# A planned one-core attention and mixer kernel: four small edits to its start, one wait, its normalisation and its last tile

## The chip, the cores and the metric

The kernel runs on one core of one Trainium2 chip. The metric is the device time of one execution in microseconds (us). A profile of an execution has a *span*, from the first to the last recorded instruction; the device time is longer than the span by 1.7 to 2 us in most runs. The engines are called PE (TensorE matrix products), PEld (its weight loads), DVE (VectorE), ACT (ScalarE), POOL (GpSimd) and SP (the queue that issues most transfers).

## The reference, cut to what matters

```python
# x: 2048 x 448, H = 16 heads of 28, N = 4 segments of L = 512 tokens, F = 1792
phi = lambda t: where(t > 0, t + 1, exp(t))
for s in range(4):
    qs, ks, vs = q[:, :, s], k[:, :, s], v[:, :, s]
    a_dot = softmax(qs @ ks.T * scale + causal_mask) @ vs
    a_mem = (phi(qs) @ M) / (phi(qs) @ z + 1e-6)      # memory of the earlier segments
    outs.append(g * a_mem + (1 - g) * a_dot)
    M, z = M + phi(ks).T @ vs, z + phi(ks).sum(...)
a = concat(outs) @ wo
u = gelu(layernorm(x).T @ w1 + b1)                    # mixes tokens: (448 x 2048) @ (2048 x 1792)
b = (u @ w2 + b2).T
out = gate * a + (1 - gate) * b                       # gate = sigmoid((x * gate_w).sum(-1))
```

## The kernel before

The kernel carries a small planner. Every instruction is registered with the engine that it may run on, a told cost in nanoseconds, a priority, and the buffers that it reads and writes. `plan()` simulates this list with the told costs and fixes, before anything runs, the order of instructions on every engine, which of two engines takes an instruction that has an `alt`, and which PSUM bank a result goes to. On the chip every engine then issues strictly in that order and waits on semaphores. So any edit to a cost, a dependency or the list of instructions can change the order of the whole program. PSUM banks 0 to 3 belong to the attention scores (after the start), banks 4 to 7 are a pool that all other products share.

```python
# start: x in tiles of 128 tokens; the first four make segment 0
load_x("SP", 0, 2)
load_x("ACT", 2, 2)
op("ACT", ... dma_start(wvx[.., D:D+1], gate_w ..), name="ldgw", ...)      # 448 elements of 2 bytes
op("SP",  ... dma_start(wk_nat, WK ..), name="ldwk", ...)
# ... cut: wq, wv, the other x tiles
warm_up(10, "warm", -1, 4300)                    # 128x512 products of zeros
warm_up(4, "warm2", P_PROJ + 0.01, 900, 5000.0)
# ... cut

def transposes(tc):                              # x^T of 512 tokens
    for half in range(2):                        # two of the four column blocks each
        # 8 PE transposes into one bank, then one copy of 1024 columns:
        # on DVE for half 0, on ACT for half 1 where tc == 0

def do_k(tc, hg):                                # k of 4 heads, 512 tokens, 4 matmuls of 512
    proj_d(wk_pad, R_wkp, hg, tc, b)
    op("ACT", ... copy of 512 columns ..., alt=("DVE", ...))
```

An attention unit is one segment and one group of four heads, each padded from 28 to 32 columns. Its scores come in three parts, f = 0, 1, 2, each followed by an exponential on ACT and a mask on POOL.

```python
def pv_unit(u):
    mb, cb = Bank("pool"), Bank("pool")
    if s > 0:                                    # phi(q) @ memory, into a pool bank
        op("PE", ... matmul(bank(mb)[:, 0:512], mst_sb[:, s-1, hg, :], phq[...]) ...,
           reads=[R_mst[s - 1], R_phq[hg][s]], writes=[bres(mb)], take=mb, name=f"mem{u}", ...)
    op("PE", fn, reads=R_P[tb] + R_v[...], take=cb, name=f"pv{u}", ...)      # exp(scores) @ v
    # DVE transposes mb and cb out of PSUM into t2; then, on all 32 columns of each head:
    dv(... t3[0] = t3[0] * oc * rb[0] ..., "oa", 668)          # 512 elements
    dv(... t3[1] = t3[1] * rb[1] ..., "om", 601)
    op("POOL", ... o = t2[:,0] + t2[:,1] ..., cost=1450)

def mm2(T):                                      # one output tile of 128 tokens
    for ft in range(NFT):                        # 14 matmuls of 448 columns
        op("PE", ... matmul(bank(b)[:, 0:D], w2c[...], uT[:, ft, :]) ...)
    op("DVE", ... outst = bank * omg + ag(T) ..., name=f"fin{T}", cost=600)  # the eviction
    op("SP", ... dma_start(out2[T*128 : T*128+128, :], outst[:, p, :]) ...)
```

The softmax here doesn't subtract the row's maximum and nothing guards it: scores larger than these inputs give would overflow.

## Time and profile before

| what | value |
|---|---|
| time | 190.52 us, median of 3 (190.13 to 190.76) |
| span of the profile | 189.0 us |
| first k projection starts | 8.28 us |
| last eviction starts | 186.15 us |
| between these two ("the middle") | 177.87 us |
| from the last eviction's start to the end of the span ("the tail") | 2.85 us |

Part 1 of the page gives each engine's busy time, its share of the span and its count of instructions:

```profile
PE 181.4 (96%) x1349; PEld 84.7 (45%) x1355; DVE 155.7 (82%) x311; ACT 136.2 (72%) x171; POOL 74.3 (39%) x93
```

PE is the limit. The timeline shows the start (columns: start, duration, engine, line, operation, shapes, count, and in brackets the idle time before it and what ended that):

```profile
start us, us, engine line op out<-in xcount [idle before <-releaser]
...
1.25 4.45 PE L524 MATMUL t<-t 128*128 128x512 bf16 x10 [1.25 <-DVE t L478]
...
5.49 1.59 PE L551 MATMUL t<-t 128*112 128x128 bf16 x16
...
6.91 1.03 PE L524 MATMUL t<-t 128*128 128x512 bf16 x4
7.11 1.02 ACT L563 ACTIVATE t<-t 112x1024 bf16<-112x1024 bf16 x1 [3.98 <-PE t L551]
...
8.28 1.02 PE L572 MATMUL t<-t 112*128 112x512 bf16 x4 [0.34 <-ACT t L563]
```

Ten warm-up matmuls, 16 transposes and four more warm-up matmuls run one after the other, then PE waits 0.34 us for ACT's long copy. The timeline of PE alone, after the first projection, is nearly gapless. These are all its lines with a wait, except two (60.66 and 128.73 us) that show 0.16 us of "issue" and no releaser:

```profile
30.75 0.39 PE L765 MATMUL t<-t 28*128 28x512 bf16 x4 [0.52 <-ACT t L774]
...
34.03 0.40 PE L765 MATMUL t<-t 28*128 28x384 bf16 x8 [0.48 <-ACT t L642]
...
38.00 0.36 PE L870 MATMUL t<-t 128*128 128x448 bf16 x1 [0.18 <-ACT t L584]
38.91 0.39 PE L765 MATMUL t<-t 28*128 28x512 bf16 x4 [0.55 <-ACT t L774]
...
105.77 0.73 PE L870 MATMUL t<-t 128*128 128x448 bf16 x3 [0.57 <-DVE t L670]
```

Four waits between 30 and 39 us are for ScalarE: 0.52 + 0.48 + 0.18 + 0.55 = 1.73 us. Scores (L765) can't be computed until the exponential (L774) has emptied the four score banks. One wait, at 105.8 us, is for VectorE's L670, which prepares the memory that a memory matmul (L788) multiplies with. The records of 6 of the 12 memory matmuls are missing in this trace, though their weight loads are there, and a missing record looks like idle time. One is missing just before 105.77 us, and one before each of the two "issue" lines, which are therefore not waits. A later run with the same order of PE, only_last_tile, has all records and shows the wait as it is:

```profile
105.34 0.39 PE L788 MATMUL t<-t 128*128 128x512 bf16 x1 [0.34 <-DVE t L670]
```

So PE waits 1.73 + 0.34 = 2.07 us in all. The table of stretches, for 24 to 40 us:

```profile
core 0: us, PE busy (x) PEld busy (x) DVE busy (x) ACT busy (x) POOL busy (x), PEclk, DMA share, GB/s
24.00:40.00 16.00, 14.27 (x102) 5.66 (x101) 15.03 (x40) 14.33 (x22) 9.44 (x12) 1.00 0.39 62
```

The PE timeline from 146 us also has this line; it shows three memory matmuls in a row, which take three of the four pool banks at once:

```profile
149.45 0.82 PE L788 MATMUL t<-t 128*128 128x512 bf16 x3
```

And the end, in the timeline:

```profile
174.79 11.32 PE L898 MATMUL t<-t 128*128 128x448 bf16 x59
...
186.15 0.68 DVE L904 SCALAR_TENSOR_TENSOR t<-t 128x448 bf16<-128x448 f32 x1 [1.96 <-PE t L898]
```

After the last matmul an eviction of 0.68 us and one transfer remain.

### The profile page before, as it was taken

Reading aid. Unit: us, or ns where it says so; the run is one execution under the profiler, and the core shown is the slowest. Engines: PE = TensorE matmul, PEld = TensorE weight load, DVE = VectorE, ACT = ScalarE, POOL = GpSimd, SP = SyncE. Lnnn points to the kernel's source line nnn. Section 1 sums busy time; section 2 is a strip of 40 time slices with the busy share of each in tenths; the row PEclk is TensorE's granted clock in tenths of the full one; section 3 lists DMA queues with packets and bytes.
Section 4 is the critical chain, followed back from the end, with each engine's and each line's share of the span. In section 5 each row is a group of like instructions: output and inputs, shape, how many; then the busy total and the mean of one; then the engine's idle time right before and its main releaser. Section 6 shows DMA issues by size and latency. Waiting matters only on the chain.

```text
span 189.0 us, 3425 instructions
## 1 busy us (share of the span) xinstructions
PE 181.4 (96%) x1349; PEld 84.7 (45%) x1355; DVE 155.7 (82%) x311; ACT 136.2 (72%) x171; POOL 74.3 (39%) x93
## 2 busy tenths in 40 slices
PE   7999998889999999999999899999999999999993
PEld 2545633334445444434445344444446444455551
DVE  1788899895999999899989998997998997872221
ACT  2276988986899989999998899986757867204100
POOL 8200027645242528364447454274570075510000
PEclk9999999999999999999999999999999999999999
DMA  5899991000955271801081514405590016655011
GB/s 163 208 318 243 294 204 28 0 3 0 245 120 140 70 183 28 222 7 28 0 225 43 152 28 121 105 24 127 147 270 1 3 51 192 176 150 164 26 49 49
DMA packets 42451, 21.75 MB, mean 115 GB/s; under 512 B 7876, under 2 KB 42436, under 8 KB 42436
## 3 DMA queue, kind: packets, MB, share of 16 engines
q1 hardware_dynamic: 41700, 21.32, 43.9%
q10 hardware_dynamic: 736, 0.23, 0.5%
q8 instruction: 10, 0.16, 0.4%
q14 instruction: 5, 0.04, 0.1%
HBM read 18.13 MB, written 1.84 MB: 106 GB/s over the span
## 4 chain that ended last, share of the span: by engine, by line
PE 80%; DVE 12%; ACT 6%; issue 1%
PE t L898 23%; PE t L870 20%; PE t L572 10%; PE t L850 7%; PE t L765 6%; PE t L628 5%; PE t L802 4%; ACT t L774 3%; PE t L524 2%; DVE t L714 2%; PE t L551 1%; ACT t L613 1%; DVE t L817 1%; DVE t L562 1%; PE t L652 1%
## 5 line engine op out<-in xcount | busy, mean ns | idle before, releaser
L774 ACT ACTIVATE t<-t 128x2048 bf16<-128x2048 f32 (+1 forms) x48 | 76.7, 1597 | 10.8 <-PE t L765 9.7
L778 POOL TENSOR_SCALAR_AFFINE_SELECT t<-t 128x512 bf16<-128x512 bf16 x64 | 49.1, 772 | 83.0 <-ACT t L774 79.9
L870 PE MATMUL t<-t 128*128 128x448 bf16 x224 | 48.0, 354 | 0.8 <-DVE t L670 0.6
L898 PE MATMUL t<-t 128*128 128x448 bf16 x224 | 45.3, 353 | 0.3 <-issue 0.2
L898 PEld LDWEIGHTS t<-t 128*128 128x128 bf16 x224 | 20.9, 98 | 20.8 <-issue 1.5
L572 PE MATMUL t<-t 112*128 112x512 bf16 x128 | 29.8, 380 | 0.3 <-ACT t L563 0.3
L870 PEld LDWEIGHTS t<-t 128*128 128x128 bf16 x224 | 20.1, 98 | 20.6 <-issue 2.5
L904 DVE SCALAR_TENSOR_TENSOR t<-t 128x448 bf16<-128x448 f32 x16 | 10.9, 679 | 14.4 <-PE t L898 14.3
L830 POOL TENSOR_TENSOR t<-t 128x512 bf16<-128x512 f32 x12 | 16.5, 1372 | 11.5 <-DVE t L828 11.5
L765 PE MATMUL t<-t 28*128 28x512 bf16 (+3 forms) x256 | 17.3, 302 | 1.7 <-ACT t L774 1.1
L572 PEld LDWEIGHTS t<-t 112*128 112x128 bf16 x128 | 11.7, 97 | 14.9 <-issue 1.0
L856 ACT ACTIVATE t<-t 128x448 bf16<-128x448 f32 x12 | 8.7, 723 | 12.3 <-PE t L850 11.9
L628 PE MATMUL t<-t 112*128 112x449 bf16 x64 | 13.5, 355 | 0.0
L765 PEld LDWEIGHTS t<-t 28*128 28x128 bf16 x256 | 5.1, 92 | 18.3 <-ACT t L774 12.3
L850 PE MATMUL t<-t 128*128 128x448 bf16 x64 | 13.3, 353 | 0.0
L836 DVE STREAM_TRANSPOSE t<-t 128x512 bf16<-128x512 bf16 x16 | 11.2, 701 | 1.7 <-POOL t L830 1.7
L817 DVE STREAM_TRANSPOSE t<-t 128x512 f32<-128x512 f32 x16 | 11.0, 698 | 1.5 <-PE t L802 1.5
L714 DVE BATCH_NORM_STATS2 t<-t 128x6 f32<-128x448 bf16 x16 | 9.4, 607 | 3.0 <-DMA t<-in_A_x_dram 2.9
L802 PE MATMUL t<-t 128*32 128x512 bf16 (+3 forms) x256 | 11.3, 302 | 0.1
L826 DVE SCALAR_TENSOR_TENSOR t<-t 128x512 f32<-128x512 f32 x12 | 11.1, 921 | 0.1
L595 DVE SCALAR_TENSOR_TENSOR t<-t 128x512 bf16<-128x512 bf16 x12 | 10.1, 845 | 0.0
L882 DVE SCALAR_TENSOR_TENSOR t<-t 128x448 f32<-128x448 f32 x14 | 8.8, 641 | 1.1 <-ACT t L877 1.1
(80 smaller groups left out, 215.6 us busy)
## 6 DMA issues: line engine op xcount, KB each, us to landing
t<-in_B_w_dram SPq DMA_DIRECT2D x7, 1024.0 KB, 6.2
t<-in_B_w_dram SPq DMA_DIRECT2D x8, 896.0 KB, 5.2
out_dram<-t SPq DMA_DIRECT2D x16, 112.0 KB, 2.3
t<-in_A_x_dram SPq DMA_DIRECT2D x3, 448.0 KB, 9.3
t<-in_A_wk_dram SPq DMA_DIRECT2D x1, 392.0 KB, 5.1
t<-in_A_wq_dram SPq DMA_DIRECT2D x1, 392.0 KB, 7.1
t<-in_A_wv_dram SPq DMA_DIRECT2D x1, 392.0 KB, 8.4
t<-in_A_wo_dram SPq DMA_DIRECT2D x4, 98.0 KB
```

The source lines that it names most:

```text
L572: last = e.matmul(bank(b)[:, 0:512], w_pad[0:CK, c, hg * 128 : hg * 128 + 128], xT[0:CK, c, tc * 512 : tc * 512 + 512], start=(c == 0), st ...
L628: last = e.matmul(bank(b)[:, 0 : D + 1], xT[0:CK, c, t * 128 : t * 128 + 128], wvx[0:CK, c, :], start=(c == 0), stop=(c == NCT - 1), skip_ ...
L714: op("DVE", lambda e: e.bn_stats(st6[:, t, :], xh[:, t, :]), reads=[R_x[t]], writes=[R_st6[t]], name=f"bns{t}", cost=512, prio=P_PROJ - 10)
L765: last = e.matmul(bank(hl)[:, c0 : c0 + w_], kT[r, hg, s * 512 + j * 128 : s * 512 + j * 128 + 128], qT[r, hg, s * 512 + 128 * j : s * 512 ...
L774: op("ACT", lambda e: e.activation(pv, ps[:, 0:4, 0:w], ACT.Exp, scale=SCALE), reads=R_bank[0:4], writes=[R_P[u % 2][f]], name=f"exp{n}", ...
L778: op("POOL", lambda e, d=d: e.affine_select(d, d, pattern=[[0, 4], [1, 128]], compare_op=ALU.is_ge, fill=0.0, base=0, channel_multiplier=- ...
L802: last = e.matmul(bank(cb)[32 * hl : 32 * hl + 32, 128 * j : 512], vaug[:, 4 * s + j, 32 * h : 32 * h + 32], pv[:, hl, c0 : c0 + w_], star ...
L817: dv(lambda e: e.transpose(t2[:, 0, :], bank(cb)[:, 0:512]), [bres(cb)], [R_tt[tb][0]], "ta", 630, use=(cb,))
L830: op("POOL", lambda e: e.tensor_tensor(o, t2[:, 0, :], t2[:, 1, :], op=ALU.add), reads=R_tt[tb], writes=[R_ob[tb]], name=f"o{u}", cost=145 ...
L850: last = e.matmul(bank(b)[:, 0:D], oT[:, hg, T * 128 : T * 128 + 128], wo_sb[:, hg, :], start=(hg == 0), stop=(hg == NHG - 1), skip_group_ ...
L870: op("PE", lambda e, st=st: e.matmul(bank(b)[:, 0:D], w1c[:, st, f2 * 128 : f2 * 128 + 128], xh[:, st, :], start=(st == 0), stop=(st == NT ...
L898: op("PE", lambda e, ft=ft: e.matmul(bank(b)[:, 0:D], w2c[:, ft, t2_ * 128 : t2_ * 128 + 128], uT[:, ft, :], start=(ft == 0), stop=(ft == ...
```

## The change

It has four parts.

- **A, the start.** wk is loaded ahead of x tiles 2 and 3, which move from ACT's queue to SP's. The transposes of segment 0 go by token half, and so do the copies and the k projections (two of 256 tokens, for each head group). One warm-up matmul fewer. The intent is that the first projections need only half of x.
- **B, one line.** The memory matmul also "reads" the second exponential of its unit, so that it isn't planned long before its bank will be emptied.
- **C, head pads.** Normalisation works on 28 of each 32 columns, 448 of 512 elements; the pads of `ob` are cleared once. The told costs fall with it.
- **D, last tile.** The last output tile is computed, evicted and stored in two halves of 224 columns, so that the final eviction and transfer are smaller.

```diff
 A    load_x("SP", 0, 2)
-     load_x("ACT", 2, 2)
+     op("SP", ... dma_start(wk_nat ..), name="ldwk", ...)
+     load_x("SP", 2, 2)
      ...
-     warm_up(4, "warm2", P_PROJ + 0.01, 900, 5000.0)
+     warm_up(3, "warm2", P_PROJ + 0.01, 680, 4000.0)
      ...   # transposes(0): parts ordered by token half; 512-column copies, three on DVE, one on ACT
-     for hg in range(NHG):
-         do_k(0, hg)
+     for t0 in (0, 256):
+         for hg in range(NHG):
+             do_k(0, hg, t0, 256)

 B    # memory matmul
-        reads=[R_mst[s - 1], R_phq[hg][s]], ...
+        reads=[R_mst[s - 1], R_phq[hg][s], R_P[tb][1]], ...

 C    # normalisation
+     op("DVE", ... memset(warm[:, 512:1024], 0.0), writes=[R_ob[1]], name="ob0", ...)
-     o3 = o.rearrange("p (b c) -> p b c", c=32)
+     o3 = o.rearrange("p (b c) -> p b c", c=32)[:, :, 0:DH]
+     n3 = [t[:, :, 0:DH] for t in t3]
-     ... "oa", 668 ...  "om", 601 ...  cost=1450
+     ... "oa", 602 ...  "om", 535 ...  cost=1280

 D    def mm2(T, c0=0, c1=D): ...       # columns c0:c1, own resource for the second half
+     def mm2_last(T):
+         mm2(T, 0, D // 2)
+         mm2(T, D // 2, D)
```

More of the change, by code (lines that the diff above doesn't have):

```diff
@@ L404, in build_kernel @@
     R_xT = [R(f"xT{t}_", 2) for t in range(4)]
+    R_xT0 = [R(f"xT0h{h}_", 2) for h in range(2)]
+    R_xT[0] = R_xT0[0] + R_xT0[1]
     R_phk = [R(f"phk{s}_", NHG) for s in range(3)]
@@ L410, in build_kernel @@
     R_kT = [R(f"kT{g}_", 4) for g in range(NHG)]
+    R_kTh = R("kTh", NHG)
     R_phq = [R(f"phq{g}_", 4) for g in range(NHG)]
@@ L418, in build_kernel @@
     R_rec = R("rec", 2)
-    R_ob, R_outst = R("ob", 2), R("outst", 4)
+    R_ob, R_outst = R("ob", 2), R("outst", 5)
     R_P = [R(f"P{u}_", 3) for u in range(2)]
@@ L435, in build_kernel @@
     load_x("SP", 0, 2)
-    load_x("ACT", 2, 2)
+    op("SP", lambda e: e.dma_start(wk_nat[0:CK], WK.rearrange("(c p) d -> p c d", p=CK)), writes=R_P[0],
+       name="ldwk", dma=True, cost=500, nbytes=401408)
+    load_x("SP", 2, 2)
     op("ACT", lambda e: e.dma_start(wvx[0:CK, :, D : D + 1], GW.rearrange("(c p o) -> p c o", p=CK, o=1),
@@ L439, in build_kernel @@
        writes=[R_gw], name="ldgw", dma=True, cost=500, nbytes=8000)
-    op("SP", lambda e: e.dma_start(wk_nat[0:CK], WK.rearrange("(c p) d -> p c d", p=CK)), writes=R_P[0],
-       name="ldwk", dma=True, cost=500, nbytes=401408)
     op("SP", lambda e: e.dma_start(wq_nat[0:CK], WQ.rearrange("(c p) d -> p c d", p=CK)), writes=R_P[1],
@@ L474, in ring_load @@
                writes=[R_slot[r]], name=f"ldw2_{j}", dma=True, cost=500, nbytes=917504)
+    P_BASE, P_ATT, P_PROJ, P_WO, P_M1, P_M2 = 0.0, 100.0, 200.0, 300.0, 400.0, 500.0
+    PRJ = (P_PROJ, P_PROJ + 1, P_M1 + 8.5, P_M2 + 4.5)
+    REL0, REL = 0.0, 0.0
     warm = ob.rearrange("p a q -> p (a q)")
     op("DVE", lambda e: e.memset(warm[:, 0:512], 0.0), writes=[R_ob[0]], name="warm0", cost=250)
+    op("DVE", lambda e: e.memset(warm[:, 512:1024], 0.0), writes=[R_ob[1]], name="ob0", cost=250, prio=P_PROJ)
     op("POOL", lambda e: e.memset(ident[:], 1.0), writes=[R_ident], name="id0", cost=200)
@@ L503, in load_wo @@
                reads=[R_wv], writes=[R_wo[hl]], name=f"ldwo{hl}", dma=True, cost=500, nbytes=100352)
-    P_BASE, P_ATT, P_PROJ, P_WO, P_M1, P_M2 = 0.0, 100.0, 200.0, 300.0, 400.0, 500.0
-    PRJ = (P_PROJ, P_PROJ + 1, P_M1 + 8.5, P_M2 + 4.5)
-    REL0, REL = 0.0, 0.0
     rr = [0]
@@ L543, in transposes, with fn @@
             b = next_bank()
-            def fn(e, half=half, b=b):
+            parts = [(ti, c) for ti in range(4) for c in (2 * half, 2 * half + 1)]
+            if tc == 0:
+                parts = [(ti, c) for c in range(4) for ti in (2 * half, 2 * half + 1)]
+            def fn(e, b=b, parts=parts):
                 tb = bank(b).bitcast(BF16)
                 last = None
-                for ti in range(4):
-                    for c2 in range(2):
-                        c = half * 2 + c2
-                        last = e.matmul(tb[0:CK, c2 * 512 + ti * 128 : c2 * 512 + ti * 128 + 128],
-                                        xh[:, 4 * tc + ti, c * CK : c * CK + CK], ident[:, :], is_transpose=True,
-                                        start=True, stop=True, skip_group_check=True)
-                return last
@@ L556, in io @@
-            def io(half=half, b=b):
-                return (xT[0:CK, 2 * half : 2 * half + 2, tc * 512 : tc * 512 + 512],
-                        bank(b).bitcast(BF16)[0:CK, :].rearrange("p (c t) -> p c t", c=2))
-            op("PE", fn, reads=R_x[4 * tc : 4 * tc + 4] + [R_ident], writes=[bres(b)], **btake(b),
-               name=f"trx{tc}_{half}", mode="f", cost=8 * 56, prio=P_PROJ)
-            on_dve = ("DVE", lambda e, io=io: e.tensor_copy(*io()), dve_cost(1024, 2))
-            on_act = ("ACT", lambda e, io=io: e.activation(*io(), ACT.Copy), act_cost(1024))
@@ L564, in transposes @@
-            first, other = (on_act, on_dve) if tc == 0 and half == 1 else (on_dve, on_act)
-            op(first[0], first[1], **buse(b), reads=[bres(b)], writes=[R_xT[tc][half]], name=f"xTcp{tc}_{half}",
-               cost=first[2], prio=P_PROJ + tc - 150, alt=other if tc else None)
-    def proj_d(w_pad, R_w, hg, tc, b):
+                for ti, c in parts:
+                    at = (c * 256 + ti % 2 * 128) if tc == 0 else (c % 2 * 512 + ti * 128)
+                    last = e.matmul(tb[0:CK, at : at + 128], xh[:, 4 * tc + ti, c * CK : c * CK + CK], ident[:, :],
+                                    is_transpose=True, start=True, stop=True, skip_group_check=True)
@@ new lines, in fn, with io @@
+                return last
+            op("PE", fn, reads=[R_x[4 * tc + ti] for ti, c in parts] + [R_ident], writes=[bres(b)], **btake(b),
+               name=f"trx{tc}_{half}", mode="f", cost=8 * 56, prio=P_PROJ + (0.02 if tc == 0 and half else 0))
+            if tc == 0:
+                for k, on_dve in ((0, True), (1, half == 1)):
+                    def io(b=b, half=half, k=k):
+                        return (xT[0:CK, 2 * k : 2 * k + 2, half * 256 : half * 256 + 256],
+                                bank(b).bitcast(BF16)[0:CK, k * 512 : k * 512 + 512].rearrange("p (c t) -> p c t", c=2))
+                    if on_dve:
+                        op("DVE", lambda e, io=io: e.tensor_copy(*io()), reads=[bres(b)], writes=[R_xT0[half][k]],
+                           name=f"xTcp0_{half}{k}", cost=dve_cost(512, 2), prio=P_PROJ - 150)
+                    else:
+                        op("ACT", lambda e, io=io: e.activation(*io(), ACT.Copy), reads=[bres(b)],
+                           writes=[R_xT0[half][k]], name=f"xTcp0_{half}{k}", cost=act_cost(512), prio=P_PROJ - 150)
+            else:
+                def io(half=half, b=b):
+                    return (xT[0:CK, 2 * half : 2 * half + 2, tc * 512 : tc * 512 + 512],
+                            bank(b).bitcast(BF16)[0:CK, :].rearrange("p (c t) -> p c t", c=2))
+                op("DVE", lambda e, io=io: e.tensor_copy(*io()), **buse(b), reads=[bres(b)], writes=[R_xT[tc][half]],
+                   name=f"xTcp{tc}_{half}", cost=dve_cost(1024, 2), prio=P_PROJ + tc - 150,
+                   alt=("ACT", lambda e, io=io: e.activation(*io(), ACT.Copy), act_cost(1024)))
@@ L569, in fn, with proj_d @@
+    def proj_d(w_pad, R_w, hg, tc, b, t0=0, n=512):
         def fn(e):
@@ L571, in fn, with do_k @@
             for c in range(NCT):
-                last = e.matmul(bank(b)[:, 0:512], w_pad[0:CK, c, hg * 128 : hg * 128 + 128],
-                                xT[0:CK, c, tc * 512 : tc * 512 + 512], start=(c == 0), stop=(c == NCT - 1),
+                last = e.matmul(bank(b)[:, 0:n], w_pad[0:CK, c, hg * 128 : hg * 128 + 128],
+                                xT[0:CK, c, tc * 512 + t0 : tc * 512 + t0 + n], start=(c == 0), stop=(c == NCT - 1),
                                 skip_group_check=True)
             return last
-        op("PE", fn, reads=R_xT[tc] + [R_w], writes=[bres(b)], **btake(b), name=f"prd{tc}_{hg}", mode="f",
-           cost=pe_cost(512, 512, 512, 512), prio=PRJ[tc])
-    def do_k(tc, hg):
+        need = R_xT[tc] if tc else [r for h in range(2) if t0 < 256 * h + 256 and t0 + n > 256 * h for r in R_xT0[h]]
+        op("PE", fn, reads=need + [R_w], writes=[bres(b)], **btake(b), name=f"prd{tc}_{hg}", mode="f",
+           cost=pe_cost(n, n, n, n), prio=PRJ[tc] + (0.01 if t0 else 0))
+    def do_k(tc, hg, t0=0, n=512):
         b = next_bank()
-        ks = kT[:, hg, tc * 512 : tc * 512 + 512]
-        proj_d(wk_pad, R_wkp, hg, tc, b)
-        op("ACT", lambda e: e.activation(ks, bank(b)[:, 0:512], ACT.Copy),
-           **buse(b), reads=[bres(b)], writes=[R_kT[hg][tc]], name=f"cpk{tc}_{hg}", cost=act_cost(512), prio=P_BASE,
-           alt=("DVE", lambda e: e.tensor_copy(ks, bank(b)[:, 0:512]), dve_cost(512)))
+        ks = kT[:, hg, tc * 512 + t0 : tc * 512 + t0 + n]
+        proj_d(wk_pad, R_wkp, hg, tc, b, t0, n)
+        op("ACT", lambda e: e.activation(ks, bank(b)[:, 0:n], ACT.Copy),
+           **buse(b), reads=[bres(b)], writes=[R_kTh[hg] if t0 else R_kT[hg][tc]], name=f"cpk{tc}_{hg}",
+           cost=act_cost(n), prio=P_BASE, alt=("DVE", lambda e: e.tensor_copy(ks, bank(b)[:, 0:n]), dve_cost(n)))
     def do_kphi(tc, hg):
@@ L590, in do_kphi @@
         ks = kT[:, hg, tc * 512 : tc * 512 + 512]
-        op("ACT", lambda e: e.activation(kphi[:, p, :], ks, ACT.Exp), reads=[R_kT[hg][tc]],
+        op("ACT", lambda e: e.activation(kphi[:, p, :], ks, ACT.Exp), reads=[R_kT[hg][tc]] + ([] if tc else [R_kTh[hg]]),
            writes=[R_kphi[p]], name=f"ek{tc}_{hg}", cost=act_cost(512, True), prio=P_PROJ + tc)
@@ L769, in fn @@
             return last
-        op("PE", fn, reads=[R_kT[hg][s], R_qT[hg][s]], writes=R_bank[0:4], name=f"sc{n}", mode="r",
+        op("PE", fn, reads=[R_kT[hg][s], R_qT[hg][s]] + ([] if s else [R_kTh[hg]]), writes=R_bank[0:4], name=f"sc{n}", mode="r",
            cost=w / 2.4 + 17, prio=pr, rel=REL0 + REL * u)
@@ L790, in pv_unit @@
                                         skip_group_check=True),
-               reads=[R_mst[s - 1], R_phq[hg][s]], writes=[bres(mb)], take=mb, name=f"mem{u}", mode="f",
+               reads=[R_mst[s - 1], R_phq[hg][s], R_P[tb][1]], writes=[bres(mb)], take=mb, name=f"mem{u}", mode="f",
                cost=pe_cost(512), prio=pr)
@@ L820, in pv_unit @@
         o = ob[:, tb, :]
-        o3 = o.rearrange("p (b c) -> p b c", c=32)
-        rb = [rec[:, tb, k, :, None].to_broadcast([128, 16, 32]) for k in range(2)]
+        o3 = o.rearrange("p (b c) -> p b c", c=32)[:, :, 0:DH]
+        n3 = [t[:, :, 0:DH] for t in t3]
+        rb = [rec[:, tb, k, :, None].to_broadcast([128, 16, DH]) for k in range(2)]
         oc = omcol[:, hg : hg + 1]
@@ L825, in pv_unit @@
             dv(lambda e: e.reciprocal(rec[:, tb, :, :], dens), R_tt[tb], [R_rec[tb]], "rec", 280)
-            dv(lambda e: e.scalar_tensor_tensor(t3[0], t3[0], oc, rb[0], op0=ALU.mult, op1=ALU.mult),
-               [R_tt[tb][0], R_rec[tb], R_omcol], [R_tt[tb][0]], "oa", 668, port=True)
-            dv(lambda e: e.tensor_tensor(t3[1], t3[1], rb[1], op=ALU.mult), [R_tt[tb][1], R_rec[tb]], [R_tt[tb][1]],
-               "om", 601, port=True)
-            op("POOL", lambda e: e.tensor_tensor(o, t2[:, 0, :], t2[:, 1, :], op=ALU.add), reads=R_tt[tb],
-               writes=[R_ob[tb]], name=f"o{u}", cost=1450, port=True, prio=pr)
+            dv(lambda e: e.scalar_tensor_tensor(n3[0], n3[0], oc, rb[0], op0=ALU.mult, op1=ALU.mult),
+               [R_tt[tb][0], R_rec[tb], R_omcol], [R_tt[tb][0]], "oa", 602, port=True)
+            dv(lambda e: e.tensor_tensor(n3[1], n3[1], rb[1], op=ALU.mult), [R_tt[tb][1], R_rec[tb]], [R_tt[tb][1]],
+               "om", 535, port=True)
+            op("POOL", lambda e: e.tensor_tensor(o3, n3[0], n3[1], op=ALU.add), reads=R_tt[tb],
+               writes=[R_ob[tb]], name=f"o{u}", cost=1280, port=True, prio=pr)
         else:
             dv(lambda e: e.reciprocal(rec[:, tb, 0, :], dens[:, 0, :]), [R_tt[tb][0]], [R_rec[tb]], "rec", 200)
-            dv(lambda e: e.scalar_tensor_tensor(o3, t3[0], oc, rb[0], op0=ALU.mult, op1=ALU.mult),
-               [R_tt[tb][0], R_rec[tb], R_omcol], [R_ob[tb]], "oa", 668, port=True)
+            dv(lambda e: e.scalar_tensor_tensor(o3, n3[0], oc, rb[0], op0=ALU.mult, op1=ALU.mult),
+               [R_tt[tb][0], R_rec[tb], R_omcol], [R_ob[tb]], "oa", 602, port=True)
         dv(lambda e: e.transpose(oT[:, hg, s * 512 : s * 512 + 512], o), [R_ob[tb]], [R_qT[hg][s]], "ot", 635)
@@ L889, in mm1, with mm2 @@
            reads=[R_gg[q], R_vh[q]], writes=[R_uT[ft]], name=f"gelu{ft}", cost=535, port=True, prio=P_BASE)
-    def mm2(T):
+    def mm2(T, c0=0, c1=D):
         b = Bank("pool")
@@ L897, in mm2 @@
         for ft in range(NFT):
-            op("PE", lambda e, ft=ft: e.matmul(bank(b)[:, 0:D], w2c[:, ft, t2_ * 128 : t2_ * 128 + 128],
-                                               uT[:, ft, :], start=(ft == 0), stop=(ft == NFT - 1),
+            op("PE", lambda e, ft=ft: e.matmul(bank(b)[:, 0 : c1 - c0], w2c[:, ft, t2_ * 128 : t2_ * 128 + 128],
+                                               uT[:, ft, c0:c1], start=(ft == 0), stop=(ft == NFT - 1),
                                                skip_group_check=True),
                reads=[R_slot[r]] + (R_uT if ft == 0 else [R_uT[ft]]), writes=[bres(b)],
-               take=b if ft == 0 else None, name=f"y{T}_{ft}", mode="f", cost=pe_cost(448),
-               prio=P_M2 + T)
-        op("DVE", lambda e: e.scalar_tensor_tensor(outst[:, p, :], bank(b)[:, 0:D], omg[:, T : T + 1], ag(T),
-                                                   op0=ALU.mult, op1=ALU.add),
-           **buse(b), reads=[bres(b), R_kT[T % 4][T // 4], R_gcol[T]], writes=[R_outst[p]], name=f"fin{T}", cost=600,
-           prio=P_BASE)
-        op("SP", lambda e: e.dma_start(out2[T * 128 : T * 128 + 128, :], outst[:, p, :]), reads=[R_outst[p]],
-           name=f"out{T}", dma=True, out=True, cost=500, nbytes=114688)
+               take=b if ft == 0 else None, name=f"y{T}_{ft}", mode="f", cost=pe_cost(c1 - c0), prio=P_M2 + T)
+        op("DVE", lambda e: e.scalar_tensor_tensor(outst[:, p, c0:c1], bank(b)[:, 0 : c1 - c0], omg[:, T : T + 1],
+                                                   ag(T)[:, c0:c1], op0=ALU.mult, op1=ALU.add),
+           **buse(b), reads=[bres(b), R_kT[T % 4][T // 4], R_gcol[T]], writes=[R_outst[4 if c0 else p]],
+           name=f"fin{T}", cost=dve_cost(c1 - c0) + 60, prio=P_BASE)
+        op("SP", lambda e: e.dma_start(out2[T * 128 : T * 128 + 128, c0:c1], outst[:, p, c0:c1]),
+           reads=[R_outst[4 if c0 else p]], name=f"out{T}", dma=True, out=True, cost=500, nbytes=256 * (c1 - c0))
+    def mm2_last(T):
+        mm2(T, 0, D // 2)
+        mm2(T, D // 2, D)
     transposes(0)
-    for hg in range(NHG):
-        do_k(0, hg)
+    for t0 in (0, 256):
+        for hg in range(NHG):
+            do_k(0, hg, t0, 256)
     pad_q()
@@ L949, in build_kernel @@
     do_mst(2)
-    mlp = [(mm1, ft) for ft in range(NFT)] + [(mm2, T) for T in range(NT)]
+    mlp = [(mm1, ft) for ft in range(NFT)] + [(mm2, T) for T in range(NT - 1)] + [(mm2_last, NT - 1)]
     for u in range(16):
```

## The prediction

> **What bounds the kernel now.** TensorE. The page's first part: PE 181.4 us busy of a 189.0 us span; the stretch table: PE 32.8 of 33.0 us from 60 to 93 us. The chain of waits is 80% PE. PE idles in four places. (1) Before the first projection at 8.28 us it does only warm-up, 16 transposes and a 0.34 us wait. (2) From 30 to 39 us it waits some 1.7 us for exponentials (L774) and other ScalarE work. (3) At 105.5 us a memory matmul (L788) waits for VectorE's L670 and PE idles 0.57 us. (4) After the last matmul, at 186.15 us, a 0.68 us eviction (L904) and one transfer take 2.85 us.
>
> **Start.** Timeline: warm-up ends at 5.70, transposes take 1.39 us of the chain, four more warm-up matmuls 1.03, then PE waits 0.34 for a 1.02 us ScalarE copy (L563). The change drops one warm-up matmul (0.26 us), splits the copies (estimate from the 512-column 0.60 us: 0.55 on ScalarE, 0.4 on VectorE) and brings wk ahead of x tiles 2 and 3. But 10 warm-up, 16 transposes and 3 warm-up matmuls still run serially: no k projection before about 7.8 us. It adds 16 matmuls, each some 8 ns beyond its columns (512 columns took 221 ns, 213 at full rate): 0.13 us; and perhaps 0.1 to 0.3 us where the fourth head group's first half reuses a PSUM bank that VectorE must first empty. Gain 0.2 to 0.5 us, expected 0.35. The Trainium skill, "TensorE: Matmul & The Clock Gate", Part 1, has the clock gate open after some 3.4 us of sustained activity; here warm-up matmuls took 445 ns at first, 257 in the second group, so one fewer should not leave the projections cold.
>
> **Memory matmul after its exp.** It stops three memory matmuls running together (149.45 us) and holding three PSUM banks, after which mm2's weight load waited 0.50 us for L817. It won't cure (3): there the exp was long done. Expected 0.2, of 0 to 0.4, with reshuffling of the static order of either sign.
>
> **Head pads.** 64 of 512 elements less: about 67 ns from each L826, L828 and L834 (28 in all), 1.9 us of VectorE's 155.7, some 2 us of GpSimd's 74.3 (L830). Mostly off the critical path: 0.1 us.
>
> **Last tile.** 28 matmuls of 224 columns for 14 of 448: same time (14 x 189 ns = 2.65 us), as 128-column matmuls ran at 56 ns each, so weight loads don't limit. The eviction falls from 0.68 to about 0.44 us. The transfer halves, but is mostly latency, and its rows are now 448 bytes, below the 512 that the skill's "DMA: Bandwidth & Descriptors", Specifications, names for line rate. Gain 0.25 us.
>
> **Sum.** 0.35 + 0.2 + 0.1 + 0.25 = 0.9 us: **189.6 us**, range 188.6 to 190.6. Chances: faster by over 2% 0.03, within 2% 0.95, slower 0.02.
>
> **What would show it.** First k projection at 7.7 to 7.9 us, k and q projections done 0.2 to 0.5 us earlier than 15.35; last eviction 0.42 to 0.47 us; L826 and L828 some 70 ns shorter; the PE wait at L670 still there; the three L788 no longer together; PE still about 96% busy.
>
> **What would make it wrong.** A PE wait over 0.5 us inside the k halves; a cold clock in the first projections; a reshuffled order with more switches between tiled and full matmuls, or new ScalarE stalls (over 1 us either way).

## The result, and the profile after

The changed kernel takes 188.69 us (median of 4, 188.43 to 188.84); the kernel before took 190.64 us on the same chip in the same rounds (median of 4, 190.13 to 190.83). A ratio in this document is the recorded one, of one kernel's fast runs over the other's of the same rounds. The quotient of the medians that stand beside it differs from it by up to 0.0016, that of the plain means by up to 0.0005. Here it is 0.99 (95% interval 0.9877 to 0.9924). The time lies within the predicted range (188.6 to 190.6), 0.09 us inside its lower end, but the gain of 1.95 us is twice the predicted 0.9 us, so the sum was wrong.

| | before | after | difference |
|---|---|---|---|
| span | 189.0 | 186.4 | −2.6 |
| first k projection | 8.28 | 7.80 | −0.48 |
| middle | 177.87 | 176.13 | −1.74 |
| tail | 2.85 | 2.50 | −0.35 |
| device time less span, profiled execution | 1.74 | 2.03 | +0.29 |

Part 1 of the page after:

```profile
PE 180.6 (97%) x1373; PEld 87.3 (47%) x1384; DVE 154.0 (83%) x319; ACT 133.5 (72%) x171; POOL 69.6 (37%) x93
```

The start in the timeline after:

```profile
5.43 0.61 PE L558 MATMUL t<-t 128*112 128x128 bf16 x8
...
5.88 0.81 PE L528 MATMUL t<-t 128*128 128x512 bf16 x3
...
6.16 0.63 DVE L536 COPY t<-t 112x1792 bf16<-112x1792 bf16 x1
...
6.70 0.42 DVE L571 COPY t<-t 112x512 bf16<-112x512 bf16 x1
...
6.77 0.65 PE L558 MATMUL t<-t 128*112 128x128 bf16 x8
...
7.15 0.60 ACT L574 ACTIVATE t<-t 112x512 bf16<-112x512 bf16 x1 [4.61 <-DVE t L571]
7.80 1.38 PE L589 MATMUL t<-t 112*128 112x256 bf16 x11 [0.38 <-ACT t L574]
```

PE still waits 0.38 us for ScalarE's copy: the two short copies read the same bank and run one after the other (the ScalarE copy is released by the DVE copy). And the first of them starts 0.66 us after the transposes that it reads (5.43 + 0.61 = 6.04 us), because VectorE's order has the copy of wk (L536) before it. The same PE timeline as before, after the first projection, now holds only these two lines with a wait, apart from two of 0.16 us "issue", each of which again stands where the record of a memory matmul is missing:

```profile
30.57 0.29 PE L783 MATMUL t<-t 28*128 28x256 bf16 x4 [0.32 <-ACT t L792]
...
143.14 0.39 PE L783 MATMUL t<-t 28*128 28x512 bf16 x4 [0.31 <-ACT t L875]
```

The 1.73 us for ScalarE between 30 and 39 us have become 0.32 us, the wait for L670's counterpart has gone, and a new one of 0.31 us has come. The stretch from 24 to 40 us agrees, with 1.4 us more of PE's time busy:

```profile
24.00:40.00 16.00, 15.68 (x112) 6.52 (x111) 15.14 (x38) 14.14 (x21) 8.42 (x11) 1.00 0.26 41
```

And the end, in the timeline:

```profile
178.40 5.50 PE L917 MATMUL t<-t 128*128 128x448 bf16 x42
...
182.59 0.45 DVE L922 SCALAR_TENSOR_TENSOR t<-t 128x224 bf16<-128x224 f32 x1 [0.66 <-PE t L917]
183.94 0.45 DVE L922 SCALAR_TENSOR_TENSOR t<-t 128x224 bf16<-128x224 f32 x1 [0.89 <-PE t L917]
```

The last eviction fell from 0.68 to 0.45 us. (In this trace 11 of the 12 memory matmuls have no record. Their weight loads show that they ran, and that no three stand together any more.)

### The profile page after: what moved, and what is told of

It is laid out like the page before. It is cut to its first block, busy times and chain, and to the rows that moved or that the text cites. A ratio compares the mean times of both kernels' runs of the same rounds, so it can differ in the third digit from the quotient of the medians.

```text
span 186.4 us, 3493 instructions
## 1 busy us (share of the span) xinstructions
PE 180.6 (97%) x1373; PEld 87.3 (47%) x1384; DVE 154.0 (83%) x319; ACT 133.5 (72%) x171; POOL 69.6 (37%) x93
## 4 chain that ended last, share of the span: by engine, by line
PE 82%; DVE 6%; ACT 6%; DMA 3%; issue 1%; SPq 0%
PE t L889 24%; PE t L917 24%; PE t L589 9%; PE t L783 7%; PE t L869 6%; PE t L820 6%; PE t L646 3%; ACT t L792 3%; DMA t<-in_A_wk_dram 3%; DVE t L732 2%; PE t L670 1%; ACT t L631 1%; PE t L558 1%; DVE t L581 1%; DVE t L624 1%
## 5 line engine op out<-in xcount | busy, mean ns | idle before, releaser
L796 POOL TENSOR_SCALAR_AFFINE_SELECT t<-t 128x512 bf16<-128x512 bf16 x64 | 47.0, 737 | 64.2 <-ACT t L792 59.9
L889 PE MATMUL t<-t 128*128 128x448 bf16 x224 | 47.3, 353 | 0.4 <-issue 0.3
L917 PE MATMUL t<-t 128*128 128x448 bf16 (+1 forms) x238 | 46.0, 342 | 0.3
L589 PE MATMUL t<-t 112*128 112x512 bf16 (+1 forms) x144 | 30.0, 356 | 0.4 <-ACT t L574 0.4
L849 POOL TENSOR_TENSOR t<-t 128x448 bf16<-128x448 f32 x12 | 14.3, 1196 | 18.2 <-DVE t L847 18.2
L589 PEld LDWEIGHTS t<-t 112*128 112x128 bf16 x144 | 13.4, 98 | 13.1 <-issue 0.9
L922 DVE SCALAR_TENSOR_TENSOR t<-t 128x448 bf16<-128x448 f32 (+1 forms) x17 | 11.1, 653 | 10.0 <-PE t L917 7.5
L875 ACT ACTIVATE t<-t 128x448 bf16<-128x448 f32 x9 | 6.6, 730 | 12.4 <-PE t L869 12.2
L869 PE MATMUL t<-t 128*128 128x448 bf16 x64 | 13.6, 353 | 0.0
L835 DVE STREAM_TRANSPOSE t<-t 128x512 f32<-128x512 f32 x16 | 11.3, 703 | 2.6 <-PE t L820 2.6
L626 ACT ACTIVATE t<-t 128x512 bf16<-128x512 f32 x8 | 4.8, 595 | 11.4 <-PE t L589 11.4
L906 DVE SCALAR_TENSOR_TENSOR t<-t 128x448 bf16<-128x448 f32 x14 | 9.2, 658 | 2.9 <-ACT t L904 2.8
```

The lines of the kernel that those rows point to most:

```text
L589: last = e.matmul(bank(b)[:, 0:n], w_pad[0:CK, c, hg * 128 : hg * 128 + 128], xT[0:CK, c, tc * 512 + t0 : tc * 512 + t0 + n], start=(c == ...
L796: op("POOL", lambda e, d=d: e.affine_select(d, d, pattern=[[0, 4], [1, 128]], compare_op=ALU.is_ge, fill=0.0, base=0, channel_multiplier=- ...
L835: dv(lambda e: e.transpose(t2[:, 0, :], bank(cb)[:, 0:512]), [bres(cb)], [R_tt[tb][0]], "ta", 630, use=(cb,))
L849: op("POOL", lambda e: e.tensor_tensor(o3, n3[0], n3[1], op=ALU.add), reads=R_tt[tb], writes=[R_ob[tb]], name=f"o{u}", cost=1280, port=Tru ...
L869: last = e.matmul(bank(b)[:, 0:D], oT[:, hg, T * 128 : T * 128 + 128], wo_sb[:, hg, :], start=(hg == 0), stop=(hg == NHG - 1), skip_group_ ...
L889: op("PE", lambda e, st=st: e.matmul(bank(b)[:, 0:D], w1c[:, st, f2 * 128 : f2 * 128 + 128], xh[:, st, :], start=(st == 0), stop=(st == NT ...
```

## The experiments

My theory: the extra gain sits in the middle and comes from the static order that the planner finds for the changed program. The rival: the parts each save their own direct cost (shorter operations, a removed wait, a better start), and these add. Twelve kernels were run; all gave correct outputs. They ran on three chips; a ratio is always to the kernel before. Kernels are compared only within the same rounds. The summary, with times in us. First k, middle and tail are from the profiled execution; the last column is the range of device time less span over all executions of the run (the spans are known to 0.1 us):

| run | parts | median | ratio (95%) | first k | middle | tail | outside span |
|---|---|---|---|---|---|---|---|
| before | – | 190.3 to 190.6 | 1 | 8.28 | 177.87 | 2.85 | 1.67–1.78, once 2.0 |
| after | ABCD | 188.69 | 0.99 (0.9877–0.9924) | 7.80 | 176.13 | 2.50 | 2.02–2.06 |
| only_k_halves | A | 193.39 | 1.0146 (1.0108–1.0183) | 7.86 | 180.91 | 2.83 | 1.77–1.87 |
| only_mem_wait | B | 189.62 | 0.9971 (0.9957–0.9985) | 7.80 | 177.07 | 2.85 | 1.71–1.77 |
| only_pads | C | 191.19 | 1.0042 (1.0021–1.0063) | 8.54 | 178.24 | 2.84 | 1.74–2.51 |
| only_last_tile | D | 190.25 | 1.0 (0.9988–1.0012) | 8.08 | 177.90 | 2.50 | 1.75–1.87 |
| halves_and_wait | AB | 188.53 | 0.9891 (0.9875–0.9906) | 7.93 | 176.09 | 2.84 | 1.77–1.83 |
| halves_wait_tile | ABD | 188.49 | 0.989 (0.9875–0.9905) | 7.98 | 176.13 | 2.49 | 1.95–2.01 |
| all_but_wait | ACD | 191.26 | 1.0035 (1.0023–1.0047) | 7.95 | 178.89 | 2.49 | 1.98–2.06 |
| pads_order_kept | C, old told costs | 190.61 | 1.0003 (0.9989–1.0017) | 8.00 | 177.89 | 2.84 | 1.68–1.79 |
| costs_only | told costs of C alone | 191.78 | 1.0054 (1.0032–1.0077) | 8.11 | 178.29 | 2.85 | 1.72–2.86 |
| order_transplant | before in AB's order | 189.61 | 0.9951 (0.9935–0.9966) | 8.64 | 175.98 | 2.86 | 1.70–2.01 |
| one_output | ABD, one last transfer | 188.32 | 0.9881 (0.9865–0.9897) | 7.79 | 176.11 | 2.61 | 1.73–1.79 |
| both_on_vector | ABD, see below | 188.0 | 0.9864 (0.9848–0.988) | 7.84 | 175.72 | 2.53 | 2.00–2.09 |

One execution of the kernel before, in the rounds of pads_order_kept, took 462 us. It counted as slow and is left out of every figure.

### One part at a time

**only_k_halves** is part A alone:

```diff
-     load_x("ACT", 2, 2)
+     op("SP", ... "ldwk" ...);  load_x("SP", 2, 2)
-     warm_up(4, "warm2", P_PROJ + 0.01, 900, 5000.0)
+     warm_up(3, "warm2", P_PROJ + 0.01, 680, 4000.0)
      # transposes(0) and copies by token half
+     for t0 in (0, 256):
+         for hg in range(NHG): do_k(0, hg, t0, 256)
```

> The kernel before with only the start changed: wk loaded ahead of x tiles 2 and 3, transposes and first k projections in halves of 256 tokens, 3 warm-up matmuls for 4. Theory 1 (start only: the gain is the earlier first projection and nothing more): 0.3 to 0.6 us faster than before, first k projection at 7.8 us, and PE still waits about 1.4 to 1.9 us in all for ScalarE between 28 and 40 us. Theory 2 (the start moves the whole static order, and with it the ScalarE waits of 28 to 40 us go): 1.2 to 2 us faster, these waits under 0.6 us. Theory 3 (every edit reshuffles the order and the rest is luck): anything from 1 us slower to 1.5 us faster, with new waits at other places.

It is slower: ratio 1.0146, some 2.8 us by the means, which none of the three theories had allowed, although its first projection starts at 7.86 us. The ScalarE waits of 30 to 39 us are gone (one of 0.31 us is left), but the PE timeline shows this in the middle:

```profile
58.08 0.81 PE L805 MATMUL t<-t 128*128 128x512 bf16 x3
...
59.34 0.36 PE L887 MATMUL t<-t 128*128 128x448 bf16 x1
61.93 0.29 PE L782 MATMUL t<-t 28*128 28x256 bf16 x4 [2.22 <-ACT t L791]
62.57 0.85 PE L819 MATMUL t<-t 128*32 128x512 bf16 x16 [0.35 <-DVE t L832]
```

Three memory matmuls (L805) run together at 58.08 us. They take three of the four pool banks; the DVE timeline shows when these are emptied:

```profile
61.76 0.67 DVE L832 STREAM_TRANSPOSE t<-t 128x512 f32<-128x512 f32 x1
...
63.04 0.70 DVE L832 STREAM_TRANSPOSE t<-t 128x512 f32<-128x512 f32 x1
```

In between PE idles 2.22 us and then 0.35 us. The trace puts the first of these down to ScalarE's exponential (L791), because the next instruction in PE's order is a score; that PE has nothing else in its order there is the planner's doing. Its plan for this kernel, calculated again without the chip, gives the three memory matmuls banks 7, 4 and 5 while an MLP tile holds bank 6, and has no MLP matmul between 57.0 and 61.0 us of its own clock; the plan of halves_and_wait, the kernel with A and B below, has 17 there. (A further wait, 0.87 us at 163.6 us, is for VectorE's output eviction, L921.) The table of stretches shows what this leads to (columns as above; the last but two is the granted TensorE clock):

```profile
59.70:62.90 3.20, 0.62 (x13) 0.36 (x16) 3.19 (x6) 3.20 (x5) 0.89 (x2) 1.00 0.56 159
62.90:66.50 3.60, 3.60 (x27) 1.10 (x18) 3.60 (x9) 2.76 (x4) 1.23 (x2) 0.53 0.60 154
66.50:70.00 3.50, 3.50 (x38) 1.65 (x37) 1.50 (x4) 2.16 (x4) 0.64 (x1) 1.00 0.19 37
```

After a stretch in which PE was busy for 0.62 of 3.20 us, the clock averaged 0.53 over 3.6 us (0.50 from 63.1 to 66.4 us), and 448-column matmuls started 346 to 374 ns apart instead of 189. This happened in 4 of the 6 executions (the clock over the span was below 1.0 in them): those took 193.38 to 194.6 us, the other two 191.89 and 191.97. So the low clock is worth about 1.5 us (2.7 us in the one execution at 194.6), and the order without it still costs about 1.6 us (191.93 against the 190.31 of before). The Trainium skill, "TensorE: Matmul & The Clock Gate", Part 1, says that the clock is halved "after ≥1 idle window (~3.4µs)". The trace agrees with the size and the time scale. But here PE was not idle for a whole such window, its longest idle stretch being 2.22 us.

**only_mem_wait** is part B alone:

```diff
-        reads=[R_mst[s - 1], R_phq[hg][s]], ...
+        reads=[R_mst[s - 1], R_phq[hg][s], R_P[tb][1]], ...
```

> The kernel before with only the memory matmul made to wait for its unit's exp. Everything before about 60 us keeps its order. Theory 1: 0 to 0.4 us faster, the three memory matmuls at 149 us no longer together, the 0.5 us PE wait for VectorE's L670 at 105 us still there. Theory 2: the same as before within 0.3 us. Theory 3: up to 1 us either way.

Ratio 0.9971, some 0.6 us by the means, a little more than the 0 to 0.4 us expected; the profiled execution, the fastest of six, has a middle 0.80 us shorter. The wait for L670 at 105.8 us is gone, against the expectation. The three memory matmuls of 149 us are no longer together, though two still are. The ScalarE waits of 30 to 39 us stand unchanged, at 1.75 us in sum. (The early first projection of its profile, 7.80 us, is not its doing: B doesn't touch the start. The starts of kernels without A vary from 7.80 to 8.54 us. The clock opened between 3.99 and 7.15 us in them, and the ten warm-up matmuls took between 3.67 and 4.45 us; where it opened early, PE waited 0.87 to 1.14 us for the copy of wk instead.)

**only_pads** is part C alone (the diff is that of C above).

> The kernel before with only the head pads left out of the normalisation (28 of 32 columns, with the lower costs told to the scheduler, which reorders). Theory 1: 0.1 us faster, the three VectorE operations each about 70 ns shorter. Theory 2: within 0.3 us of before. Theory 3: up to 1 us either way, by waits at other places than before.

It is slower by 0.42%, although it only takes work away.

**only_last_tile** is part D alone (the diff is that of D above). It keeps PE's order of the kernel before.

> The kernel before with only the last y tile in two column halves. The order of all else is the same, so all theories expect the same: 0.25 to 0.4 us faster, from the last eviction (0.68 to about 0.45 us) and perhaps 0.1 us from the smaller transfer; last matmul ends at the same time as before, within 0.1 us.

The tail in the span fell by 0.35 us, as in the changed kernel, but the time did not change: 1.0, from 0.9988 to 1.0012. The expected 0.25 to 0.4 us did not come.

What follows: the parts don't add. The four ratios sum to 1.6% slower, and the changed kernel is 1.0% faster. Even with only the executions of A that kept the clock, 0.8% slower, the sum is 1.0% slower. The rival theory falls.

### Parts together

**halves_and_wait** is A and B:

> The kernel before with the start changed and the memory matmul made to wait for its exp; pads and last tile as before. Theory 3a (the halves alone are slow because, in the order they lead to, memory matmuls for later units take three of the four free PSUM banks early and leave PE nothing to do; the wait cures just that): 1.3 to 2 us faster than before, no PE wait over 0.6 us, clock 1.0, although the halves alone measured 1.5% slower and the wait alone 0.3% faster. Additive theory: 1 to 2 us slower than before.

```diff
      # A as in only_k_halves, and
-        reads=[R_mst[s - 1], R_phq[hg][s]], ...
+        reads=[R_mst[s - 1], R_phq[hg][s], R_P[tb][1]], ...
```

Ratio 0.9891, so these two parts alone give the whole gain of the change. A alone costs 1.5%, B alone gives 0.3%, both together give 1.1%. No wait is over 0.6 us, as the theory said; its PE timeline has just one after the first projection:

```profile
30.70 0.29 PE L782 MATMUL t<-t 28*128 28x256 bf16 x4 [0.32 <-ACT t L791]
```

**halves_wait_tile** is A, B and D, the same with `mm2_last` of D added. **all_but_wait** is the changed kernel with B's line undone:

```diff
-               reads=[R_mst[s - 1], R_phq[hg][s], R_P[tb][1]], ...
+               reads=[R_mst[s - 1], R_phq[hg][s]], ...
```

> The whole change without the pads part (full 32 columns in the normalisation). It has the order of the run of halves and wait, with the last tile split. If the pads part is worth 0.1 us or more in the whole change, this is slower than the whole change (188.69 us) by that; if the pads part acts by its reshuffled order, this is 0 to 0.6 us faster than the whole change: 188.1 to 188.7 us. Against the run of halves and wait of the same call it should be 0.25 to 0.4 us faster, by the last eviction and transfer; if the tile is really worth nothing, as alone, equal.

> The whole change without the memory matmul's wait. Theory 3a: 1 to 3 us slower than before, with a PE wait of about 2 us near 60 us behind three memory matmuls run together, and, where that wait is long enough, a stretch of halved TensorE clock after it in some runs. Additive theory: at most 0.6 us slower than the whole change, so about 189.2 us.

D adds nothing to A and B (0.989 against 0.9891). Without B the gain turns into a loss of 0.35%, with the clock at 1.0 in all runs. That is less than the 1 to 3 us expected, and the wait of about 2 us near 60 us did not come: only two memory matmuls run together there. The PE timeline of all_but_wait shows smaller waits for VectorE; three of them:

```profile
64.35 1.31 PE L889 MATMUL t<-t 128*128 128x448 bf16 x6 [0.23 <-DVE t L833]
...
75.14 0.93 PE L869 MATMUL t<-t 128*128 128x448 bf16 x4 [0.39 <-DVE t L899]
...
78.74 1.04 PE L589 MATMUL t<-t 112*128 112x512 bf16 x4 [0.81 <-DVE t L835]
```

L833 and L835 are the transposes that empty memory and attention banks. So the traces and plans fit the intended mechanism of B, to keep banks from being held long before VectorE can empty them, and B is worth far more beside A than in the kernel before. These listed waits are too short to account for the whole loss (see the sums below), and B's line also moves the rest of the order, so how much of the loss is held banks is not shown.

### The order alone

To tell the order from everything else that A and B change, **order_transplant** takes the instructions of the kernel before, unsplit and with its own transfers, and gives them the order (and the choice of engine) that the planner found for halves_and_wait. Three head groups' first k projections stand at the start, and the fourth's, whole, where the split order had its second half, at about 18 us.

```diff
+ORDER = {"PE": "warm.0 trx0_0.0 warm2.0 trx0_1.0 prd0_0.0 ...".split(), "ACT": ..., ...}
      def plan(self):
-            for e in o.alts: ...
+            bisect.insort(waiting[at[o.idx]], ...)           # engine as listed
-            if o.take is None or any(...)
+            if uid[o.idx] == todo[e][0] and (...)            # only the next one on the list
```

> The instructions of the kernel before, all of them, at the start as well (full k projections, four warm-up matmuls, no added wait), but issued on every engine in the order that the run of halves and wait had. If the gain of the middle is the order's alone: 1.2 to 2 us faster than before (188.6 to 189.4), with under 0.8 us of PE waits for ScalarE between 24 and 40 us, and at most 0.4 us slower than the run of halves and wait, for the later first projection. If the halved projections themselves are needed: within 0.5 us of before. The scheduler's own estimate is against the order theory here (0.2 us slower than before).

Ratio 0.9951, some 0.9 to 1.0 us faster: less than the 1.2 to 2 us expected, and further behind halves_and_wait (0.9891) than the 0.4 us allowed. Its profiled middle is 175.98 us, against 176.09 of halves_and_wait and 177.87 of before, but the profiled execution is the fastest of its six (189.2 us, the others 189.42 to 189.84). By the means its span is 1.06 us shorter than that of before (187.80 against 188.86). If the later first projection, 8.64 us instead of 8.28, costs all of them the same, the middle gains about 1.4 us; this is an estimate. So with the instructions of before, the order alone gives most of the gain of the middle, 1.4 to 1.9 us of some 1.8; whether the split projections themselves add something is not decided. What it lacks besides is the start, since the borrowed order was made for short copies. Its PE timeline:

```profile
8.64 5.34 PE L698 MATMUL t<-t 112*128 112x512 bf16 x24 [1.21 <-DVE t L840]
...
31.61 0.29 PE L891 MATMUL t<-t 28*128 28x256 bf16 x4 [0.48 <-ACT t L900]
...
148.73 0.29 PE L891 MATMUL t<-t 28*128 28x256 bf16 x4 [0.22 <-ACT t L900]
```

(The second of the lines after the start stands where the record of a memory matmul is missing, so I don't count it as a wait.) A check on this reading is the sum of all waits that PE's timeline shows after 9 us, beside the middle, without what missing records explain. For the kernel before I take only_last_tile, which has the same order and all records:

| | before's order | B | A and B | order_transplant | after | C | A, C and D |
|---|---|---|---|---|---|---|---|
| waits on PE, us | 2.07 | 1.75 | 0.32 | 0.48 | 0.63 | 1.89 | 2.17 |
| middle less these waits, us | 175.83 | 175.32 | 175.77 | 175.50 | 175.50 | 176.35 | 176.72 |

In the first five the rest is the same to within about half a microsecond, and the middles differ mostly by their waits. In the two slow orders it is not: 0.5 to 1.4 us more of their middles lie outside the listed waits. Such a list misses short stalls, since the records of 448-column matmuls last 353 ns though the next one can start after 189 ns, so a stall of up to some 0.16 us does not show. Why does this order wait less? In the kernel before the first scores run at 22.15 us and exponentials of up to 1.9 us each then compete on ScalarE with the copies of the second segment's projections. In halves_and_wait the first scores run at 24.45 us, when more of these projections are done, and between 34.4 and 40.9 us 29 matmuls of the MLP stand between the scores, so that PE has work while ScalarE finishes. I read this from the two timelines; it was not varied by itself.

### Where the loss of the pads came from

**pads_order_kept** has the narrow operations of C with the old told costs, so that the planner finds the old order (PE's order is exactly that of before). **costs_only** is the opposite: the operations of before, with the told costs of C. Its order is exactly that of only_pads.

```diff
 pads_order_kept, against only_pads:
-   ... "oa", 602 ...  "om", 535 ...  cost=1280
+   ... "oa", 668 ...  "om", 601 ...  cost=1450
 costs_only, against before:
-   ... "oa", 668 ...  "om", 601 ...  cost=1450
+   ... "oa", 602 ...  "om", 535 ...  cost=1280
```

> The kernel before with the normalisation on 28 of 32 columns but with the old costs told to the scheduler, so that every engine keeps the order of before (VectorE has one memset more at the start). Direct theory: 0 to 0.2 us faster than before, L826, L828 and L834 some 70 ns shorter each. If the pads alone were slow (0.4% slower) because strided operands are slow, this is slower than before too; if because of the new order, it is not.

> The instructions of before, unchanged; only the costs told to the scheduler for the four normalisation steps are lowered as in the change, so that the order is exactly that of the pads alone. Order theory: 0.3 to 0.6 us slower than before (ratio 1.002 to 1.004), as the pads alone were. If the pads alone were slow because of their operands: equal to before.

The narrow operations by themselves are worth nothing: 1.0003 (0.9989 to 1.0017). And they did get shorter. From the groups of VectorE (after the bar: busy us, mean ns of one; then the idle time before), first before, then pads_order_kept:

```profile
L826 DVE SCALAR_TENSOR_TENSOR t<-t 128x512 f32<-128x512 f32 x12 | 11.1, 921 | 0.1
...
L828 DVE TENSOR_TENSOR t<-t 128x512 f32<-128x512 f32 x12 | 9.7, 806 | 0.0
```

```profile
L828 DVE SCALAR_TENSOR_TENSOR t<-t 128x448 f32<-128x448 f32 x12 | 10.2, 848 | 0.1
L830 DVE TENSOR_TENSOR t<-t 128x448 f32<-128x448 f32 x12 | 8.6, 719 | 0.0
```

These 73 and 87 ns, 12 times each, lie on an engine that PE rarely waits for (the four of L834 lost 181 ns each, and GpSimd's twelve 137 ns). The three numbers told to the planner, without any change of an instruction's work, made the kernel slower: 1.0054 (1.0032 to 1.0077), somewhat more than the 1.002 to 1.004 expected. The instructions being the same, this is the order's doing, and so is the loss of only_pads. How the order does it is only partly explained. Of the 1.02 us by which the mean of costs_only exceeds that of before, 0.32 us lie in the span (the profiled middle is 0.42 us longer) and 0.70 us outside of it: in 4 of its 6 executions the time outside the span was 2.69 to 2.86 us instead of 1.7. What that is stays open.

### Where the gain of the last tile went

In only_last_tile 0.35 us less of tail left no gain. Means over the executions show two reasons. The time outside the span grew, by 0.11 us in only_last_tile (1.82, against 1.71 for the kernel before with its one odd 2.0 left out) and by 0.18 us from halves_and_wait to halves_wait_tile (1.80 to 1.98). And the spans fell by less than the tail, by 0.09 us (188.61 to 188.52) and 0.20 us (186.73 to 186.53). The starts of one kernel's executions differ by a few tenths of a microsecond, so with four or five of them I don't read more into the difference between these and 0.35 us.

**one_output** is halves_wait_tile with a single transfer of the whole row after the second half:

```diff
-        op("SP", ... dma_start(out2[.., c0:c1], outst[:, p, c0:c1]), ...)
+        if c1 == D:
+            op("SP", ... dma_start(out2[.., :], outst[:, p, :]),
+               reads=[R_outst[p]] + ([R_outst[4]] if c0 else []), ...)
```

> Halves, wait and split last tile, but the last tile leaves in one transfer of whole 896-byte rows after both evictions. In runs with the split transfer the time outside the profile's span was about 2.0 us, without it 1.7 to 1.8. If the 448-byte rows or the extra transfer cause that, it is 1.7 to 1.8 us here; the span's tail after the last matmul should be 2.6 to 2.7 us (2.53 with two transfers, 2.88 with an unsplit tile). Sum: 0.1 to 0.2 us faster than the run of halves, wait and tile, so ratio to before 0.988.

The tail in the span is then 2.61 us, still 0.24 us less than before, and the time outside the span is back at 1.73 to 1.79 us. The ratio is 0.9881, against 0.989 for halves_wait_tile in other rounds; the intervals overlap, so whether this is better in total isn't decided. What is shown is that leaving in two transfers instead of one costs about 0.2 us after the last record, which takes back a good half of what the smaller eviction and transfer give in the tail.

**both_on_vector** joins two ideas: both copies of the first token half on VectorE, so that the ScalarE copy doesn't stand in the chain, and the last tile cut at 192 columns, so that the last transfer has rows of 512 bytes.

```diff
-                for k, on_dve in ((0, True), (1, half == 1)):
+                for k, on_dve in ((0, True), (1, True)):
-        mm2(T, 0, D // 2);  mm2(T, D // 2, D)
+        mm2(T, 0, 192);     mm2(T, 192, D)
```

> Halves, wait and split last tile, with both copies of the first token half on VectorE (the ScalarE copy waited for the VectorE copy of the same PSUM bank), and the last tile split at 192 columns so that the last transfer has 512-byte rows. Expected: first k projection at 7.5 to 7.7 us instead of 7.9, time outside the span back at 1.75 us if the row length matters and 2.0 if not; 0.2 to 0.6 us faster than the run of halves, wait and tile (188.49), if the new order brings no new wait: 187.9 to 188.3 us, ratio to before about 0.987.

It is the fastest kernel, 188.0 us (187.9 to 188.11), ratio 0.9864, faster than the changed kernel too by the medians. But not for the reason I gave: the first projection came at 7.84 us and not at the expected 7.5 to 7.7. In that execution x landed late (the first statistics of x started at 5.09 us) and the first eight transposes ran at the low clock (1.03 us). The wait before the projection did fall to 0.16 us. The gain is in the middle, 175.72 us: once more another order. And the time outside the span stayed at 2.0 to 2.09 us. So it isn't the row length of the last transfer that costs. What the slower endings share is a second transfer for the last tile; they also all have rows under 512 bytes in its first transfer (384 or 448 bytes), which no run took apart, and the mechanism stays open.

## Why the prediction was right or wrong

The time was in the range, and "within 2%" was right. The sum was not: 0.9 us were predicted, 1.95 us came. That the time still fell into the range, by 0.09 us, is partly luck: it came by an effect that was not in the sum, with two of the priced gains (pads, last tile) missing.

- **The middle, the term that was mis-sized.** "Memory matmul after its exp … Expected 0.2, of 0 to 0.4, with reshuffling of the static order of either sign." The middle gave 1.74 us. The prediction priced B as a local wait and the order as noise. The runs show that the order is the effect: the order of A and B on the old instructions gives most of the gain of the middle (1.4 to 1.9 us), A's order without B loses 1.5%, and B's line alone gains 0.3%. The possibility was named last ("a reshuffled order … over 1 us either way"), but it was not in the sum.
- **The mechanism of B** was right: "It stops three memory matmuls running together … and holding three PSUM banks". In the changed kernel no three stand together. The profile and the plan of only_k_halves show the held banks at 58 us, at a far higher price than in the kernel before, 2.22 us of idle PE and a halved clock.
- **"It won't cure (3)", "the PE wait at L670 still there": wrong.** The wait, 0.34 us without the missing record, is gone, with B alone as well; but it is gone with C alone too, so another order is enough, and B's line is not what it takes.
- **The four ScalarE waits** were listed as place (2) where PE idles, and no gain was expected there. They fell from 1.73 to 0.32 us. A's order does this: it is so in every kernel with A (0.31 to 0.41 us left), and it stays so with unsplit projections in that order (0.48 us).
- **Start.** "Gain 0.2 to 0.5 us, expected 0.35": the mean first projection of six kernels without A is 8.14 us (before, B, C, D, pads_order_kept, costs_only), that of six with A (all except both_on_vector) 7.89 us, so about 0.25 us. "No k projection before about 7.8 us" holds, to 0.01 us. The feared wait for a bank inside the halves didn't come: 40 matmuls ran in 5.82 us without a gap. But the planner moved the fourth head group's second half to about 18 us, so my test by the end of the k and q projections means nothing. The prediction missed that x itself lands later with A: the transfer of its first two tiles lands at 4.79 to 5.07 us, against 3.68 to 4.01 us in kernels without A, though it is issued at the same 0.8 us, and tiles 2 and 3 land at 6.72 us in the kernel after instead of 4.10. (From 1.8 to 4.1 us the transfers moved 288 GB/s in the kernel before and 104 GB/s after.)
- **Pads.** "Mostly off the critical path: 0.1 us." The operations shrank about as predicted; worth 0.
- **Last tile.** "The eviction falls from 0.68 to about 0.44 us" (0.45), "same time" of the matmuls (95 to 96 ns for each 224-column one, twice 14 of them), "Gain 0.25 us": in the span it was 0.35 (0.23 by the eviction, 0.12 by the transfer, which landed in 1.54 instead of 1.66 us), in the time 0. Time outside the profile's span took back some of it; the rest is below what the runs resolve. The fear of rows below 512 bytes, from the Trainium skill, "DMA: Bandwidth & Descriptors", Specifications, did not show: the 448-byte rows landed in 1.5 us, no later than 512-byte rows.
- **"PE still about 96% busy"**: 97%.

## What to carry to other kernels

Where a planner fixes a static order, measure an edit's order apart from its work: put the new order on the old instructions, or the old order on the new ones, and never add up parts measured singly. When PE is the limit, list its waits over the whole profile first, before and after; here their sum explained most of the gain of the middle (though not the losses of the slow orders), while shorter VectorE operations explained nothing. Before calling a gap a wait, check by the weight loads that no matmul record is missing there. And check a gain at the end of a program on the device time, since a shorter span can be paid for after the last record.

## What the Trainium skill lacked or had wrong

- "TensorE: Matmul & The Clock Gate", Part 1, ties the halved clock to at least one idle window of about 3.4 us. Here the granted clock averaged 0.53 over 3.6 us after a stretch in which PE was busy for 0.62 of 3.20 us and idle for at most 2.22 us at a time. The clock fell in 4 of 6 executions of the same kernel, at a price of about 1.5 us. A later section of the page lets frequent shorter pauses re-throttle too, but gives no length for them.
- No page says that the device time exceeds the profile's span by an amount that depends on the program's end: with part A, 1.73 to 1.87 us with one transfer for the last tile and 1.95 to 2.09 us with two; and in costs_only either 1.7 or 2.69 to 2.86 us, for unknown reasons.
- "DMA: Bandwidth & Descriptors", Specifications, names 512 bytes as the least for line rate, and lacks what this means for a single small transfer. Output transfers with 448-byte rows (56 KB) landed in 1.5 us, and so did ones of 64 KB with 512-byte rows and of 48 KB with 384-byte rows. At this size no run shows a penalty; since all three took the same time, they don't test the rate.
- No page that I used explains why the first two x tiles landed 1.1 us later (4.79 instead of 3.68 us) when tiles 2 and 3 moved to the same queue and the transfer of 448 elements of 2 bytes became the first on the other one. "Trainium Kernel Development and Optimization", Key Constraints, says that using several queues only saves issue time; the x transfer was issued at 0.80 us in both, yet from 1.8 to 4.1 us all transfers together moved 104 instead of 288 GB/s. No run here took this apart.
